# Three weight loads held back in the prologue, GpSimd's chunk products cut into pieces, and a new instruction order: delta-rule attention followed by SwiGLU on one core

## The chip, the core and the metric

The kernel runs on one core of a Trainium2 chip. Its time is device microseconds (us) from start to end of one execution. The time before is a median of 677.06 us over 3 runs (677.0, 677.06 and 680.48). The instructions are named by the engine that runs them: PE (TensorE), ACT (ScalarE), DVE (VectorE), POOL (GpSimd) and SP, which here only issues transfers.

## What is computed

```python
# q, k, v: (4, 8, 768, 48), beta: (4, 8, 768)
k_n = k / (norm(k, axis=-1) + 1e-6)
state = zeros((B, H, 48, 48))
for t in range(768):
    y[:, :, t] = q_t @ state                        # read before the write
    state = state + beta_t * outer(k_t, v_t - k_t @ state)
x = y.transpose(0, 2, 1, 3).reshape(3072, 384)
xn = x / sqrt(mean(x * x, axis=-1) + 1e-6) * rms_g
g = xn @ w_gate                                     # 384 x 1536
out = (g * sigmoid(g) * (xn @ w_val)) @ w_out       # 1536 x 384
```

The loads of w_gate, w_val and w_out find 64-bit numbers in HBM (the tiles that they land in are declared I64), so a weight tile is twice as large on the way in as in use and is converted to float32 on the chip.

## The kernel before

**Chunks.** The 768 steps are cut into 12 chunks of 64. For every chunk `prep(c)` builds the inverse of a triangular matrix of the keys, `recur(c)` uses it to get the chunk's outputs and the next state, and the feed-forward part (`ffn_plain` for chunks 0 and 1, `ffn` with fewer and smaller matmuls for the others) turns the normalized outputs into 256 rows of the result. `recur` of one chunk needs the state that the one before left. The feed-forward part depends on nothing later, so it is the filling that PE works through while the chain of small steps goes on beside it.

**Chunk 0** has nothing to hide behind. `invert(0)` (its merge levels are the two rounds n = 0 and 1 at lines 761 to 799) goes through transposes on DVE, 64-row matmuls mw (line 771) and mxt (line 790), and small products on ACT and DVE: the first level writes `wx` on DVE (line 784), the second on ACT (line 782). Then come mr0 (line 1102), the output matmuls pu (line 1082), the squares for the norm on ACT (line 1164), the root on POOL (line 1189), the scaling (lines 1200 and 1204), the turn of the result (line 1215) with its copy into xp1 (line 1224), and the first matmul of the feed-forward part (line 1287). Where the plan sees PE idle in this stretch, `run` puts matmuls of the identity in (line 1550), so that PE is not idle for long. Some 128-row work stands among the 64-row matmuls on purpose (`dense`, line 779).

**Weights.** `weights(first, last)` loads 18 tiles of 768 KB (n = 0 to 17; line 371) into seven landing buffers `raw`, and converts each: two ACT instructions (lines 469 and 470), two on DVE (lines 464 and 467). RAWS (line 291) says which buffer a tile lands in: n = 4, 5, 6 in raw 4, 5, 6; n = 7 to 9 in raw 0 to 2 again; n = 10 in raw 5. A buffer takes its next tile only when both ACT conversions of its last one have read it. Tiles 0 to 3 (HELD = 4) are planned before chunk 0's inverse; the rest after it. Raw 4 is held: a one-element POOL copy writes it from `wx[0]` (line 1502), and the load of tile 4 has to come after that write.

**Order.** Nothing is scheduled at run time. `P.add` numbers the operations in the order in which the program names them, with the engine, a planned duration and the tiles read and written; dependencies follow from these. The string ORDER (line 30) holds the order in which they are issued, two characters for each number. Every engine has its own queue, in order, and so has SP for the loads. The planned durations and start times no longer choose the order: they only place the fillers and hand out the eight PSUM banks, of which each matmul group holds one from its first matmul to its last reader.

**The long products.** For chunks 4 to 11 `prep` has `fast = False`: the scaling of the 128 x 1024 tile `at` by beta (line 846), the first shared product (line 871) and the sum (line 876) go to POOL, one instruction each. The steps of the inverse behind them (lines 893 and 899) run on DVE, as do the last operations of every feed-forward product (lines 1392 and 1399).

**The table.** A Silu of two numbers (line 404) stands in ACT's order ahead of all others, so that the table that Silu needs is loaded there.

Of the kernel before, what the change touches and what calls it, by code (L numbers as in the profile page):

```python
# [9 lines left out]
FP32 = mybir.dt.float32  # L10
U32 = mybir.dt.uint32
I64 = mybir.dt.int64
ALU = mybir.AluOpType
# [17 lines left out]
    "#.#'#-#$#3#)#4###,#/#&#0#>#`#W#C#^#a#T#_#X#U#k#(#Y#w#Z#d#l#b#n#m#e#o#V#t#H#c#+#2#@#u#f#*#[#]#v#r#x#S#p#y#R#z#?#1#{#E"  # L31
    "#M#|#q#=#}#i#s#~#j$##D$$%/$'$($%#A$&$*#%#J$.$/$)$+$0#F$,$1%0$I$2%1$-%2#G$7$6$5$3$8$;$N#I$<#h$X#N$C#K$=$D%4$>$9#P$?$:"
    "#L$S%5$B#O#g%8%7%6$4%;%:%9#B%=%<%>$@%G%?%@%H%Q$J%I%3%J%B%A%T%L%K$O%C%M%D%F%c%O%N%W%E%P%U&=%X&O&C%V&>#6$K#Q%Y%S$c$Q$P"
    "#9&G$E$^$R$A%Z&H$F%^%R$G%_&D$H$T$L&I'0&E%`%[&F$U&2&J%]$Y$m%a&K$d&1%b$Z&P&3%d&L%e$M&U&M%f$_&*%g&Q&)&N#:$V$h&R$[%h&0%i"
    "&V$r&S$`$a$W&W'1$w$]&Z&X&T$e$b&[&+$|%j$i%k&`%l&]$f%n&Y'2&4&a$g$s%m&e&^%o$j&,%p&b%%&-%q'_&_$k%r&.$n$l$o%w%v$x%*%s&j$u"
    "$t(3%x$z$}%y$y%t%z&c&/$v'+%u'O&%%|&5&&&$#<${'P(2%}'R'.$~&f%#%,$p%{&g'Q$q%$%~&h&6'S','/&'%'&#&d'-'T&((:'M&i'3#8'L'U#7"
    "'V'6#;%&&7&k'8'7'Z%+'Y(4&p%-#5'4'X'5%.'W'9(5&q(6%(&8)+'I':(7';&l%)'<'[&r'J&o),&m'='K&n&t'>&s(8)8&z'?)9'@)-'`']'E).*O"
    "'A&u):&A'N&{)l&v&|'B'^)o&y)p&w'C&~'D&x&}'a)m'#'b'c)n'F'd'G'$'e'f)q'('g'H)I'%)s)/)r(C'h)w'i&?(O(D')'j'&(G'*(E'k'')v(H"
    "(F(9'l*N(K'm(I&B)u'n(L&@'o)t(P(J'p(Q'q&9'r(R's(M(U(S't(N(V)0'u)1'w(Z(T'x)K(;'v([)y)2)x(W)E'|(]);(#(X)J(Y(`)3(^()){)<"
    "(*(a(')4)|($)F'~(e(_(%)z(b'}(()}'{)L(c(&)=(A(+)~'y(f*#(,(?*$'z*%(-&:(d(g*&)M(B(/(0*'*U(1(<(.(h*((@)N)O*V(i*)(k)P*P**"  # L40
    "(l&;*+(p(m)Q(=(n(q*Q*,(u(r*R(s(v(>*-*S(j(w*.(o*/&<*0(z*1*T)R*2(x,7*3({)S*4)k)T,8)>,:*6,9(t)j*8,;)?*5)U)5,<*7)V)6)G)W"
    "(y,=,>*W(~)Y,B(|)X,?)@)_,A(})Z)A)`)#,@)[)a*E)b)]*B)^)$)c*F)d*>)e)f+q)g,C)h)i,D)7*X*[)%*C)B*G*D*`)H,v*H*9*b*a)C*A*d)D"
    "*c+r)(*f+s*e)**Z,E,F*h)&*g*<,G*l*Y*@*=*i*n*:,H*m*j*?*r*o)'*I,},I*p*v,J))*;+.,w*q*s,K*t*J*^,L*M*w*x,M*K*u*~,N*L+w*y,O"
    "+t*_,P*]+&,x,~*k+x+u*z+'+v+0+#+(,y+2+1,z+)+**{+3,Q+/+6,{+$+y+4++,R+,+:*|+-+z+5+7*},|+<+%+;._+@+=+B+{+A+|+D,S+C+F,T+E"
    "+~.`,U+L+>+8+}+G.b.a+H+M,#.c,6+P-#,$+T+Q.d+I+R,%,V-$+N+J+S.e,*+U.f,&+O+]+V+9.h,'+K,+,(+W-),)+?.j,W+_.g+^+X,,.i+Z-',X"
    "+c,Y+Y,Z+[+`,-.l,5+a,[,.,^,/+e.<,_+b+d,0,`+g.>,]+f.k,1,2+i,3,4,m-++j-&--,j-,-%-*-/+h,f,g-1.m-0,n-.,i-U-2.n+l-7,k.o/A"
    "-9-8,c.p,l,o-:/B-3,p+k.q+m,e.r-4,h,a,b.s,q,d+n.t-5-=+p,s.=+o,u.u-A,t-(-;,r-6-?->.v-C.w-@.B-B.x.?.y-E-D.@/C.C-I-F-M-J"
    "-W-<-K-N-Q.z-O-G-X-Y-P-L-V/D-^-Z/E.D-[/J.A-b/F-].E-_-c.{-j-R-h-H-S/G-k-d-T.F1*.G.(-e.H.|.I-i-l.J.}-f-n.~.L.K1+/#-m-p"
    "-`-o-t-a-q1--u-x-r1,/$-|1.-y-v.M-g-z.Q-}.N/K.O-w.R.P-{-~-s1/.)/%.S.T.#.*.&11.$10.%/&.'14.U...^13/'15/I.V.+.,/+./.112"
    ".W/).0.4/(.-/M/*.X.Y.2.5.Z16.[171j/R.3/9.]/T/6/V/U.6/S.8/P19/7/H1:/X/W/0.918/Z/Y/3/_.:/[.;/a/`.71;/8/}/b/Q/g/L1</-1="  # L50
    "/./e/1/h/i/4/f1>/2/m1?/N/j1@/,/k/51A///:/n0g/;1B/o/O0d/l1i/<1C/u0h0e/@0f/q/>/=/v/c0#/?/d/r1p0%0$1D1q/w0j/x/p/~/y0k/]"
    "0l0'/^/s1E0&0)1k0(0i0-/z0*0m/{1l0+1m0.030n/|1n0/0,4404/t1)050o00090p1F06070q0:0;010r081o020C1G0?0<3Q0O0D0@0E0=1H0t0s"
    "3R1I3T3S0G1(3U0F0y0A0H0u3V0>0v0I0B0J3/0M3W0K0z0Q3X0L0P1J0w3Y0{3Z0W0U3]0N3[1K451L0S0R0X1M0V3_1N0[0T0|0x1Q0}0~1O1#0Y1$"
    "3^1%1&1R0]1'1P311z1r1|1{301x0Z1~1}1Y1_2$2#1T0`3`1U2%1]1[1v2*3a1a2&0a3b1`0_2,2'1^3c1s2+1S0b1y323d1u1V3e1b2-0^1W2H1c0c"
    "3f2.1w203g1Z3h1d1X21224;1t3i26233j33241h2728253k1e2@1f1g3l342<2(2A2J2)2B2=352C2/2I2L3m2K2>2D2946362P2:2E2M372N2?472F"
    "2T2G482O382Q493n2V2U2Z2W2]2;2[4=2R2_2^392a4A4:2`3o4C2c3:5y2g3O3<2d4>3;2b2X3=2h5z5|3p5{2k3>3P3?2o2l2e2i3@2p3D2w3q3E3F"
    "5}2S3A2q2j3B3r3G5~2m3C2n2f5V2Y6#2s2x2y6$2r2t6%2u2v6&3H2}6(3I2z3s6'4<3J3t2{3K3u3L3M3N3#6)4E2|4?3v4G5W3$4I3w3y3%4H3z2~"
    "3x6*3'3&4@4J4$4Q4#3(5X4%4F4M4R3|6,3}4p3*6-4K4,3~6+3+3)4L4+4N4D4(4S3,6.4'3.4W4T4*4-4B6/4X604[4&4U3-4r3{4]614)4Y6]624V"
    "6d4^634Z6[4d4s644.6c4O4`4_4P4/4e4h6542414t434a404i5Y4u664j5]5Z4k4f674|4q5[6e4b4v5_6^4x5^6k4w4l4}4~6_5`4m5#4n6l4y5$6i"
    "5(4o4c6`4g5&685)6a5*5a5'5b5.695+4z5,5c6:5d525-5e6f6b53568D5f5w5g5/5:57505l545;8E5h5%8G8F515B6;5i8H5<5x585=5j5m6<5n8%"  # L60
    "5k5o4{558I595>5C5D5p8J5@8K6=5?8O5H8M5E5q5A8N6>8L5r6j7~5s5t6?5F6g6@5u8P5v6h6A6m8$5G5I5K6o6D6B8#6q5J6C5N6E8Q5L5O6n6H6p"
    "7;5M908S6R6s6P6r6u6S8T6M8R6y9'6G5R6z6N6t6O8U5P6v6{5Q5S9(6T8V6|6Q7#8W6J6}6L6U7%6w5U7$8X5T7=6~6I8Y6K7'8Z9.6V6x7(6F8[7)"
    "948&7&8]7/6X6W7>7*7?6Z8^6Y738'7@708(74718_7775767+9)8)8`7G7<8*7C7H7A789*797O728+7:9+7B7D9,7,7I8,7-7M7P;O7J7E7U8a7N7Q"
    "8B7.7S9-7R8-:l7j8.7T7V8b7W7Y8/7F7K7^7X807Z:m7L7[7_:o817b828c7`:n877c83:p917f7d887a89:q847]858d868:7k7l7e:s8;:r8<7h8="
    ":u7g7p:w8e:t7i:v8>8?967n8@9/7m8A8f8g987o928h:y9:7s:x7q9<7r7v8i8l7t8k7w998j9;8m:z9c957u8C9=;N9>9D9@9E8x8n7z9?:{8u9A8z"
    "93:|7x9F8v8p:}9J8w9G8{9e8s9H:~7{7y;#9N7}8y9g9O9I8t;$9B8|7|;%9K8o9L9C978}9f;&9P8r8q;'9V9M9h9Q9R9o9S9Z9W9p8~9[:I;(9$9]"
# [161 lines left out]
def kernel(  # L228
# [207 lines left out]
    def weights(first, last):  # L436
# [14 lines left out]
        for n, (dst, src, keys) in list(enumerate(todo))[first:last]:  # L451
# [4 lines left out]
            dma(rdst, src, 2 + 2 * n, w=[("raw", i)], dur=0.7, work=3.06, after=WAFTER[n] if n < len(WAFTER) else 0.0)  # L456
# [21 lines left out]
    WAFTER = (4.0, 6.0, 11.0, 17.0, 20.0, 25.0, 28.0, 31.0)  # L478
# [321 lines left out]
    def prep(c):  # L800
# [44 lines left out]
        def scale():  # L845
            eng.tensor_tensor(out=at_, in0=at_, in1=bt[:, None, :].to_broadcast([128, W, W]), op=ALU.mult)  # L846

        P.add(e_, 1.27 if fast else 2.4, scale, pi, r=bkeys, w=[("at", 0), ("at", 1)])
# [21 lines left out]
        def share1():  # L870
            eng.tensor_tensor(
                out=pair, in0=at_[:, :, 0:W:2], in1=diag[:, None, :].to_broadcast([128, W, W // 2]), op=ALU.mult
            )

        def share2():
            eng.tensor_tensor(out=at_[:, :, 1:W:2], in0=at_[:, :, 1:W:2], in1=pair, op=ALU.add)

        def share3():
            for side in (0, 3):
                a1 = acc[0:64, side].rearrange("p i t -> p (i t)")  # L880
                eng.tensor_tensor(
                    out=a1[:, 1 : 1 + 34 * 15 + 1 : 34], in0=a1[:, 0 : 34 * 15 + 1 : 34], in1=diag[0:64], op=ALU.mult
                )

        P.add(e_, 1.17 if fast else 1.7, share1, pi, r=[("at", 0), ("at", 1)], w=xkeys)
        P.add(e_, 0.3 if fast else 0.5, share3, pi, r=[("at", 0), ("at", 1)], w=["acc"])
        P.add(e_, 0.69 if fast else 1.3, share2, pi, r=xkeys, w=[("at", 0), ("at", 1)])
        for j in range(0, W - 2, 2):
# [94 lines left out]
    def recur(c):  # L983
# [107 lines left out]
        def uk(h):  # L1091
            return [("u", bb, p) for bb in range(2) for p in h]
# [493 lines left out]
```

## Time and profile before

| | |
|---|---|
| median of the runs (lowest, highest) | 677.06 us (677.0, 680.48) |
| the profiled execution | 680.87 us; its span, first to last instruction, 679.2 us |
| busy, PE / DVE / ACT / POOL | 666.1 / 527.4 / 307.1 / 139.8 us |
| granted PE clock, mean | 0.992 |
| first matmul of the feed-forward part | at 46.25 us |
| end of PE's last matmul | 674.98 us |
| PE idle after 46.25 us | 0.26 + 1.63 + 0.17 + 1.31 + 0.18 + 1.49 us |
| L846 on POOL, 8 times | 2.36 us each |
| L871 and L876 on POOL, 8 times each | 1.76 and 1.30 us each |

In the views quoted below, a line of the timeline has the start in us, the time that the instructions took together, the engine, the line of the kernel, the operation, what it writes and reads, and how many were merged; in brackets stands the idle time before it and what ended that. SPq is SP's queue of transfers. A line of a table by stretch has the stretch, its length, the busy time and number of instructions of each engine, the granted clock of PE, and the share of time and rate of the transfers. A line of the waits has the waiting instruction, what it waited for, the total in us, how often and the longest. PE counts as busy with the identity matmuls too, so a busy PE in the first 46 us tells little.

### The profile page before, as it was taken

The page shows a single profiled execution, that of the slowest core. Times are in us where ns is not written, and L with a number is a line of the kernel's source. Part 1 is how long each engine was busy: PE and PEld are TensorE (multiplying, and loading weights), DVE is VectorE, ACT ScalarE, POOL GpSimd, SP SyncE. Part 2 cuts the span into 40 slices and gives each one's busy share as a digit, 9 for nine tenths or more (in the row PEclk, how much of TensorE's full clock was granted, in tenths as well). Part 3 has the DMA queues.
Part 4 walks back from the last instruction along what each step waited for, and adds up shares of the span by engine and source line. Part 5 has one row for each costly group of instructions (what it writes and reads, how often), then busy time and mean ns, then how long its engine had stood idle before and what let it go on. Part 6 is the DMA issues. An engine that isn't in the chain of part 4 may idle for free. (4 is left out here: it accounts for less than half of the span.)

```text
span 679.2 us, 23221 instructions
## 1 busy us (share of the span) xinstructions
PE 666.1 (98%) x10028; PEld 616.6 (91%) x10028; DVE 527.4 (78%) x1132; ACT 307.1 (45%) x744; POOL 139.8 (21%) x146
## 2 busy tenths in 40 slices
PE   8999999999999999999999999999999999999997
PEld 5688887887799999999899999999999989999997
DVE  5859978899899699589589689689679669956463
ACT  5566743133445345355255255255255254244330
POOL 2120341004321312312311403403403030000000
PEclk9979999999999999999999999999999999999999
DMA  9929752873732511831711650630721450040101
GB/s 219 277 73 259 251 117 28 156 131 89 125 44 52 103 23 28 142 60 26 122 33 25 114 91 4 117 56 16 125 51 23 68 98 3 10 72 2 24 1 25
DMA packets 216119, 55.73 MB, mean 82 GB/s; under 512 B 205200, under 2 KB 208272, under 8 KB 215696
## 3 DMA queue, kind: packets, MB, share of 16 engines
q1 hardware_dynamic: 214976, 54.05, 40.3%
q8 instruction: 79, 1.29, 0.8%
q10 hardware_dynamic: 1040, 0.20, 0.2%
q14 instruction: 24, 0.20, 0.1%
HBM read 42.94 MB, written 15.20 MB: 86 GB/s over the span
## 5 line engine op out<-in xcount | busy, mean ns | idle before, releaser
L1382 PE MATMUL bank<-xf,w_in 128*128 128x128 f32 x1440 | 180.0, 276 | 1.7 <-ACT tmp L1394 1.5
L1392 DVE TENSOR_TENSOR tmp<-tmp,bank 128x512 f32<-128x512 f32 x180 | 120.9, 684 | 67.2 <-PE bank L1382 54.3
L1382 PEld LDWEIGHTS bank<-xf,w_in 128*128 128x128 f32 x1440 | 169.7, 192 | 3.4 <-ACT tmp L1394 1.7
L1382 PE MATMUL bank<-xf,more 128*128 128x128 f32 x960 | 125.0, 277 | 1.8 <-DVE tmp L1392 1.6
L1382 PEld LDWEIGHTS bank<-xf,more 128*128 128x128 f32 x960 | 115.6, 192 | 4.3 <-DVE tmp L1392 2.0
L1394 ACT COPY tmp<-bank 128x512 f32<-128x512 f32 x120 | 68.7, 585 | 101.7 <-PE bank L1382 70.0
L899 DVE TENSOR_REDUCE acc<-acc 128x30 f32<-128x90 f32 (+4 forms) x150 | 70.9, 473 | 5.1
L1398 ACT ACTIVATE tmp<-tmp 128x256 f32<-128x256 f32 x120 | 48.1, 415 | 58.0 <-DVE tmp L1392 57.7
L597 POOL TENSOR_TENSOR knrm<-ksum,half 128x16 f32<-128x16 f32 x11 | 32.5, 2959 | 193.7 <-DVE ksum L576 193.7
L1439 PE MATMUL bank<-wo_sb,hf 128*128 128x192 f32 x360 | 63.7, 328 | 0.0
L1439 PEld LDWEIGHTS bank<-wo_sb,hf 128*128 128x128 f32 x360 | 58.1, 190 | 0.4
L1399 DVE TENSOR_TENSOR hf<-tmp 128x256 f32<-128x256 f32 x120 | 50.7, 445 | 7.4 <-ACT tmp L1398 6.9
L893 DVE TENSOR_TENSOR acc<-acc,at 128x60 f32<-128x60 f32 (+4 forms) x150 | 51.7, 345 | 2.8 <-DVE acc L899 0.5
L919 POOL COPY acc<-acc 128x128 f32<-128x128 f32 x40 | 19.3, 512 | 117.1 <-DVE acc L899 116.5
L1287 PE MATMUL bank<-xp,w_in 128*128 128x256 f32 x144 | 34.0, 383 | 0.3 <-ACT xp L1224 0.3
L1269 PE MATMUL bank<-wo_sb,hf 128*128 128x384 f32 x96 | 34.1, 488 | 0.0
L1287 PE MATMUL bank<-xf,w_in 128*128 128x256 f32 x144 | 33.4, 383 | 0.0
L846 POOL TENSOR_TENSOR at<-at,beta_b 128x1024 f32<-128x1024 f32 x8 | 18.9, 2362 | 65.2 <-DMA at<-dkk 65.2
L1287 PEld LDWEIGHTS bank<-xf,w_in 128*128 128x128 f32 x144 | 26.9, 190 | 5.2 <-issue 0.2
L1287 PEld LDWEIGHTS bank<-xp,w_in 128*128 128x128 f32 x144 | 26.7, 190 | 5.4 <-ACT xp L1224 0.5
L1239 DVE TENSOR_TENSOR xf<-xf 128x256 f32<-128x256 f32 (+1 forms) x70 | 25.6, 400 | 3.6 <-ACT xf L1224 3.2
L1448 DVE TENSOR_TENSOR tmp<-tmp,bank 128x192 f32<-128x192 f32 x30 | 10.5, 351 | 22.2 <-PE bank L1439 22.2
(204 smaller groups left out, 1025.8 us busy)
## 6 DMA issues: line engine op xcount, KB each, us to landing
at<-dkk SPq DMA_DIRECT2D x20, 256.0 KB, 3.6
vt<-in_v_dram SPq DMA_DIRECT2D x24, 192.0 KB, 4.8
out_dram<-tmp SPq DMA_DIRECT2D x48, 96.0 KB, 2.2
k<-in_k_dram SPq DMA_DIRECT2D x23, 192.0 KB, 4.8
more<-in_moe_w_gate_dram SPq DMA_DIRECT2D x4, 768.0 KB, 8.3
more<-in_moe_w_out_dram SPq DMA_DIRECT2D x4, 768.0 KB, 8.3
dkk<-kk SPq DMA_DIRECT2D x40, 64.0 KB, 2.6
q<-dq SPq DMA_DIRECT2D x20, 128.0 KB, 3.2
```

Source lines behind the costliest of these rows:

```text
L597: P.add("POOL", 2.95, lambda: nc.gpsimd.tensor_tensor(out=knrm[i2], in0=ksum[i2], in1=half, op=ALU.pow), pn, r=[("ksum", i2), "half"], w=[ ...
L893: nc.vector.tensor_tensor(out=acc[:, 1:3, 0:n, j + 2 : W].rearrange("p a i t -> p i a t"), in0=acc[:, old, 0:n, j : j + 2, None].to_broadc ...
L899: nc.vector.tensor_reduce(out=acc[:, new, 0:n, j + 2 : W], in_=acc[:, lo : lo + 3, 0:n, j + 2 : W].rearrange("p a i t -> p i t a"), axis=A ...
L1239: P.add("DVE", V(128 * n), lambda dst=dst, a=a, b_=b_, op=op: nc.vector.tensor_tensor(out=dst, in0=a, in1=b_, op=op), pxv, r=[("xp", 0)], ...
L1269: nc.tensor.matmul(po[p].t[:, 0:DM], hf[:, spot(f), 128 * p : 128 * p + 128], wo_sb[:, spot(f)], start=(f == f0), stop=(f == f1 - 1), skip ...
L1287: nc.tensor.matmul(ps.t[:, TOK * side : TOK * side + TOK], w_in[:, side, h_, 3 * t + i_, n : n + 128], x_[:, 2 * t : 2 * t + 2].rearrange( ...
L1382: nc.tensor.matmul(g.t[:, 128 * z : 128 * z + 128], fac[:, side, 128 * f : 128 * f + 128], xf[:, xs], start=(begin and z == 0), stop=False ...
L1392: P.add("DVE", V(512), lambda t=t, g=g: nc.vector.tensor_tensor(out=t, in0=t, in1=g.t, op=ALU.add), -1, r=[g], w=[tk], last=g)
L1394: P.add("ACT", A(512), lambda t=t, g=g: nc.scalar.copy(t, g.t), -1, r=[g], w=[tk], last=g)
L1398: P.add("ACT", A(256), lambda t=t: nc.scalar.activation(out=t[:, 0:256], in_=t[:, 0:256], func=ACTF.Silu), -1, w=[tk])
L1399: P.add("DVE", V(256), lambda t=t, f0=f0, p=p: nc.vector.tensor_tensor(out=hf[:, spot(f0) : spot(f0) + 2, 128 * p : 128 * p + 128], in0=t[ ...
L1439: nc.tensor.matmul(g.t[:, 0:192], a_[:, f], b_[:, f], start=(begin and f == 0), stop=(f == 5), skip_group_check=True)
```

## The change

1. **Holds.** Tiles 4, 5 and 6, and not 4 alone, are held, and until `wx[1]` of the second merge level is written, not `wx[0]`: three one-element POOL copies in place of one. The earliest planned times of the loads from tile 4 on (WAFTER) are dropped.
2. **Pieces.** The scaling and the first shared product of chunks 4 to 11 are cut into four POOL instructions of a quarter of the rows j each, the sum into two halves: 7 more instructions for each of 8 chunks. Chunks 2 and 3, whose products run on DVE, keep one instruction each.
3. **Planned durations.** Those of pu, ku, the squares, the root and the loads are changed. They move fillers and banks only.
4. **Order.** ORDER is a new string for the 2761 operations (2703 before). Read out by number and engine, its beginning says:

| queue | before | after |
|---|---|---|
| SP, after tile 3 and chunk 1's q | tiles 5, 6, 8, 4 (held), 7, 10, 9, 12 | tiles 8, 9, 4, 6, 5 (the three held), 7, 10, 11, 14 |
| ACT, from chunk 0's squares to x1 | two half conversions (one each of tiles 5 and 6, line 469) stand between the squares, the scaling and the copies into xp1 | one half conversion (tile 4) and one copy of chunk 1's turned keys stand there |
| ACT, the Silu of line 404 | ahead of chunk 0's merge levels, after the first conversion | behind the first seven Silus of the feed-forward part |
| ACT, from xp1 to the first Silu (line 1295) | 2 key copies, 5 half conversions, 4 other copies | 1 key copy, 6 half conversions |
| PE, chunk 0 | mw, mxt, mr0, pu, ku in this order | the same, with the turns of q and of chunk 1's keys at other places |
| PE, after the first feed-forward matmuls | the product of chunk 1's q with the state (line 1005) after 4 half products of the feed-forward part | after 9 of them and one down product |
| POOL | tile 4's copy, 2 roots of chunk 0, the scaling of chunk 1's keys | 3 copies, the scaling of chunk 1's keys, the 2 roots |

The diff without the strings of ORDER:

```diff
-            dma(rdst, src, 2 + 2 * n, w=[("raw", i)], dur=0.7, work=3.06, after=WAFTER[n] if n < len(WAFTER) else 0.0)
+            dma(rdst, src, 2 + 2 * n, w=[("raw", i)], dur=0.7, work=3.06 if n < HELD or n == 8 else 2.3, after=WAFTER[n] if n < len(WAFTER) else 0.0)
...
-    WAFTER = (4.0, 6.0, 11.0, 17.0, 20.0, 25.0, 28.0, 31.0)
+    WAFTER = (4.0, 6.0, 11.0, 16.0)
...
-        def scale():
-            eng.tensor_tensor(out=at_, in0=at_, in1=bt[:, None, :].to_broadcast([128, W, W]), op=ALU.mult)
-
-        P.add(e_, 1.27 if fast else 2.4, scale, pi, r=bkeys, w=[("at", 0), ("at", 1)])
+        def scale(j0, j1):
+            eng.tensor_tensor(out=at_[:, j0:j1], in0=at_[:, j0:j1], in1=bt[:, None, :].to_broadcast([128, j1 - j0, W]), op=ALU.mult)
+
+        pieces = (0, W) if fast else (0, 8, 16, 24, W)
+        for j0, j1 in zip(pieces, pieces[1:]):
+            P.add(e_, 1.27 if fast else 0.64, lambda j0=j0, j1=j1: scale(j0, j1), pi, r=bkeys, w=[("at", 0), ("at", 1)])
...
-        def share1():
+        def share1(j0, j1):
             eng.tensor_tensor(
-                out=pair, in0=at_[:, :, 0:W:2], in1=diag[:, None, :].to_broadcast([128, W, W // 2]), op=ALU.mult
+                out=pair[:, j0:j1], in0=at_[:, j0:j1, 0:W:2], in1=diag[:, None, :].to_broadcast([128, j1 - j0, W // 2]), op=ALU.mult
             )
...
-        P.add(e_, 1.17 if fast else 1.7, share1, pi, r=[("at", 0), ("at", 1)], w=xkeys)
+        for j0, j1 in zip(pieces, pieces[1:]):
+            P.add(e_, 1.17 if fast else 0.56, lambda j0=j0, j1=j1: share1(j0, j1), pi, r=[("at", 0), ("at", 1)], w=xkeys)
         P.add(e_, 0.3 if fast else 0.5, share3, pi, r=[("at", 0), ("at", 1)], w=["acc"])
-        P.add(e_, 0.69 if fast else 1.3, share2, pi, r=xkeys, w=[("at", 0), ("at", 1)])
+        pieces = pieces[::2] if len(pieces) > 2 else pieces
+        for j0, j1 in zip(pieces, pieces[1:]):
+            P.add(e_, 0.69 if fast else 0.72, lambda j0=j0, j1=j1: share2(j0, j1), pi, r=xkeys, w=[("at", 0), ("at", 1)])
...
-            P.add("PE", 0.49 * len(h), lambda h=h: pu(h), py, r=ptk + uk(h), w=gy, ps=gy, size=64 * len(h))
+            P.add("PE", 0.55 * len(h), lambda h=h: pu(h), py, r=ptk + uk(h), w=gy, ps=gy, size=64 * len(h))
...
-            P.add("POOL", 1.1 if c else 0.65, root, py, r=["half"], w=[(k_, i2, p) for p in h for k_ in ("ms", "rs")])
+            P.add("POOL", 1.1 if c else 0.85, root, py, r=["half"], w=[(k_, i2, p) for p in h for k_ in ("ms", "rs")])
...
-    t = raw[RAWS[HELD]].bitcast(FP32)[:, 0:1]
-    P.add("POOL", 0.2, lambda: nc.gpsimd.tensor_copy(out=t, in_=wx[:, 0, 0, 0:1]), 28, r=[("wx", 0)], w=[("raw", RAWS[HELD])])
+    for n in range(HELD, 7):
+        t = raw[n].bitcast(FP32)[:, 0:1]
+        P.add("POOL", 0.15, lambda t=t: nc.gpsimd.tensor_copy(out=t, in_=wx[:, 1, 0, 0:1]), 29, r=[("wx", 1)], w=[("raw", n)])
     weights(HELD, len(RAWS))
```

## The prediction, as it went on record

> **What bounds the kernel.** First the page and the waits of PE. PE is busy 98% of the span, the granted clock falls once, early, and PE waits seldom:
>
> ```profile
> PE 666.1 (98%) x10028; PEld 616.6 (91%) x10028; DVE 527.4 (78%) x1132; ACT 307.1 (45%) x744; POOL 139.8 (21%) x146
> PEclk9979999999999999999999999999999999999999
> PE bank L1382 <- DVE tmp L1392: 1.6, 1, 1.6
> PE bank L1382 <- ACT tmp L1394: 1.5, 1, 1.5
> PE bank L947 <- issue: 1.3, 1, 1.3
> PE bank L771 <- issue: 1.2, 1, 1.2
> ```
>
> Until 46.25 us PE follows chunk 0's chain; the rest of its work there is filling. From 46.25 to 674.96 it idles 5.04 us in all, so 623.7 us of matmuls stand in line there, and the change removes none of them. The time can move in three places only: the start of the feed-forward part, the 5.04 us, and 4.2 us of tail. So next I read the prologue's timeline and a table by stretch:
>
> ```profile
> 19.59 2.52 SPq L371 DMA_DIRECT2D wsum<-in_moe_w_gate_dram  x1
> 22.15 0.49 SPq L371 DMA_DIRECT2D wsum<-in_moe_w_val_dram  x1
> 22.74 0.43 SPq L371 DMA_DIRECT2D more<-in_moe_w_out_dram  x1
> 25.37 2.05 PE L790 MATMUL bank<-kk,x2bd 64*64 64x32 f32 x64
> 28.87 0.30 PE L771 MATMUL bank<-mt,m1bd 64*64 64x32 f32 x3
> 30.35 1.23 PE L771 MATMUL bank<-mt,m1bd 64*64 64x32 f32 x29 [1.17 <-issue]
> 32.65 3.63 PE L790 MATMUL bank<-kk,x2bd 64*64 64x32 f32 x64
> 46.25 1.56 PE L1287 MATMUL bank<-xp,w_in 128*128 128x256 f32 x6 [0.28 <-ACT xp L1224]
> ...
> 24.13:27.55 3.42, 3.42 (x100) 3.05 (x98) 3.39 (x8) 0.00 (x0) 0.71 (x1) 1.00 1.03 324
> 27.55:30.96 3.41, 2.24 (x57) 1.92 (x54) 3.26 (x7) 2.08 (x3) 2.33 (x2) 1.00 0.92 327
> 30.96:41.20 10.24, 10.24 (x200) 9.40 (x200) 4.42 (x9) 2.95 (x9) 0.00 (x0) 0.50 0.46 161
> ```
>
> In the middle of 32 equal matmuls of L771 PE stands for 1.17 us for nothing that a semaphore explains ("issue"). One packet of the instruction queue is in the trace just then: 16 KB, at 27.81 to 28.90 us. Transfers fill 1.03 and 0.92 of the time around it: tiles 5, 6 and 8, issued at 19.59 to 22.74. My reading: PE's next instructions were queued behind weights. In the stretch of the stall PE is busy 2.24 of 3.41 us, and for the next 10.24 us its clock is 0.50: the same 64 matmuls of L790 take 2.05 us before and 3.63 us after.
>
> **The parts, on the profiled execution's time** (680.87 us, which is the span of 679.2 and 1.67 around it).
>
> *Holds.* In the new order SP sends tile 8 as soon as raw 1 is converted, tile 9 when raw 2 is (about 25 us by ACT's rows), and then waits for `wx[1]`. So two tiles move where three did, and most of the time before 28 us is free for the instruction packet. I take the stall as gone: -1.2. If it goes, PE fills that stretch as it fills 24.13 to 27.55, where the clock stays 1.00; so the half clock goes as well. L790 3.63 to 2.05 is -1.6; mr0 (L1102, 64 instructions) 3.5 to the 2.0 that chunk 1's take at 89.86, -1.5; pu (L1082) 2.05 to 1.15 (chunk 1's at 94.59), -0.9; pieces around them -0.2. Together -4.2. Bounds: 0 if the clock falls anyway, -5.4 if both go.
>
> The added wait: behind tile 4 on SP stand tiles 6, 5, 7 and 10 and chunk 2's keys; who waits for tile 4 is ACT's conversion, which the new order puts in front of the scaling of chunk 0's output (L1204). `wx[1]` should be ready near 31 us, the POOL copies take 0.18 each. A tile issued into an empty queue lands about 4 us later (estimate: issue at 47.98, and in 50 to 52 us the transfers run at 391 GB/s, 2.0 us for each 768 KB). So tile 4 lands near 35 us, and ACT comes to it near 37. Hidden, with 1.5 to 2 us to spare; the others land every 2.0 us, for conversions after 41 us. POOL's two extra copies (0.36) fall in its 11.75 us of idle time ahead of L1189.
>
> *Order of the prologue.* ACT has one half conversion fewer (0.9) and one key copy more (0.55) between the squares and x1: -0.35. DVE's first steps come some 0.25 us later (the zeros for the queries' padding and the side sums stand behind the key sum); I take it as inside this term's error of 1 us.
>
> *The Silu of line 404* goes behind seven real ones, so the table load moves with it to the first of these. Now it is free: ACT waits for DVE's `gam` there.
>
> ```profile
> 12.47 1.28 ACT L404 ACT_TABLE_LOAD   x1
> 13.76 0.20 ACT L404 ACTIVATE rs<-mhalf 128x2 f32<-128x2 f32 x1
> ...
> 48.00:50.00 2.00, 2.00 (x69) 1.82 (x60) 0.84 (x1) 2.00 (x4) 0.00 (x0) 1.00 0.38 55
> 50.00:52.00 2.00, 2.00 (x11) 1.75 (x10) 1.86 (x5) 2.00 (x5) 0.00 (x0) 1.00 1.08 391
> ```
>
> Then it lands where ACT is busy without a gap (2.00 of 2.00). After the first feed-forward matmul PE has ten more feed-forward steps of 1.3 us and L664 (1.1), 14.1 us, before the product L1005, which needs both state copies and two banks; ACT has by then about 17 conversions and copies at 0.85 and ten small operations at 0.3 to 0.5, some 14.6 us, and 15.9 with the load. I take +1.3 (its row); bounds 0 if ACT is ahead, 2.0 if PE waits the whole difference. The Trainium skill ("ScalarE: Activation LUTs", What ACT_TABLE_LOAD costs) gives 1.28 us for the load and 1.38 more for a drain; here the next ACT instruction starts 1.29 us after the load, so the trace shows only the first. By the page's 2.66 the sum below would be 674.7.
>
> *Pieces.* The two waits of L1382 have one cause:
>
> ```profile
> 552.24 2.36 POOL L846 TENSOR_TENSOR at<-at,beta_b 128x1024 f32<-128x1024 f32 x1 [15.29 <-DMA at<-dkk]
> 552.31 2.58 DVE L1399 TENSOR_TENSOR hf<-tmp 128x256 f32<-128x256 f32 x1
> 555.40 1.37 DVE L1399 TENSOR_TENSOR hf<-tmp 128x256 f32<-128x256 f32 x1
> 557.44 0.82 PE L1382 MATMUL bank<-xf,w_in 128*128 128x128 f32 x5 [1.49 <-ACT tmp L1394]
> ```
>
> A DVE product of 0.42 us (median of 120) takes 2.58 while the long POOL product runs; ACT, then PE, wait behind it. At 176.67 the sums of L1347 stretch the same way beside L846, and PE waits 1.63. In pieces of 2.36/4 = 0.6 us DVE can get in between: -(1.63 + 1.49) = -3.1. Bounds: 0 if the lost turns come back elsewhere. Seven more starts for each chunk cost POOL at most 0.22 us each (two 16-element L881 take 0.44), 1.5 us in a period of 51 of which it is idle 37; they delay only the inverse of a later chunk. The 1.3 us at L947 is another "issue" wait; I leave it.
>
> *Planned durations* move fillers and banks: nothing measurable.
>
> **Sum:** -1.2 - 4.2 - 0.35 + 1.3 - 3.1 = -7.55; 680.87 - 7.55 = **673.3 us**. The median, 677.06, is 3.8 below the profiled execution, close to the 4.2 of the half clock, so I think that the runs at 677.0 had no such stretch: they would be at 676.7 by these terms. Against the median the gain is then only 3.7 us, 0.55%, just past the 0.5% (3.4 us) that a measurement of this kernel can tell from no change.
>
> **Rivals.**
>
> *The clock falls or the packet is late anyway.* Tile 9 may still be moving when the packet is due, and mr0 and pu are 64-row matmuls. Then 4.2 to 5.4 come back: 677.5 to 678.7. For it: the same kernel ran both at 677.0 and 680.5. Against: it fell right after the stall's stretch, and with 64-row work at full speed (24.13 to 27.55) it didn't. The Trainium skill ("TensorE: Matmul & The Clock Gate", What's actually happening) has the clock halve after an idle window of about 3.4 us; by that rule a stall of 1.17 us is no cause, and removing it brings back nothing of the 4.2, this rival's 677.5. The trace speaks against the rule: PE was never idle longer than 1.41 us before. Chance 0.15.
>
> *The pieces move no time:* DVE's lost turns are made up of more, shorter ones, or the new order has waits of its own of that size, of which the profile of before can show nothing. 673.3 + 3.1 = 676.4. For it: in 8 chunks only these two waits of PE came of 8 long products, so most are hidden. Against: both stretched products show the cause. Chance 0.18.
>
> *The hold blocks ACT,* the slower side: tiles 4, 6, 5 and 7 are issued together; if they land together, that is at 31.5 + 2 + 4 x 2.0 = 41.5 and not 35. For it: with a full queue the page's median to landing of a 768 KB tile is 8.3 us. ACT would stand before L1204 from 37 to 41.5, PE with it: +4.5, and a PE idle that long would lose the clock, +4.2: 682.0. It costs from a landing after 37 us, and makes the kernel slower than 680.4 from about 40. Against: in order of issue, tile 4 lands first. Chance 0.12.
>
> **How the numbers follow.** Forecast 0.52, own range 670.5 to 675.6: without the table's 1.3 and with L947's 1.3 gone it is 670.7; with 2.0 for the table and half of the pieces 675.6. About three quarters of it (0.40) lie under 673.7, where faster begins; the rest (0.12), the clock or packet (0.15) and the pieces (0.18) make same 0.45; the hold (0.12) and both small rivals at once (0.03; 673.3 + 4.2 + 3.1 = 680.6) make slower 0.15. The range takes the forecast's lower end and reaches over 676.4 and 678.7: 670.3 to 679.5; it leaves out the slower cases and little else.
>
> **What would show it.** The clock at 9 in all slices, no "issue" wait at L771; L1287's first start near 40.5; a table load of 1.28 us ahead of L1295 and a wait of 1 to 2 us at L1005; L846 32 times at 0.6 us, no L1399 over 1.1 us, and PE's waits at L1382 under 0.5 us. Wrong if PE starts the feed-forward part after 44 us, or if ACT's idle time names a DMA of tile 4.

## The result and the profile after

The changed kernel takes 682.51 us (median of 6 runs, 681.25 to 683.38); in the same rounds the kernel before took 677.56 us (6 runs, 677.0 to 680.58). The ratio is 1.0062, with an interval from 1.0038 to 1.0087: slower by 0.6%, where 0.55% faster was forecast. The profiled execution took 682.63 us, span 680.9. Before's profiled execution (680.87 us, mean clock 0.992) was one of its slower ones: of the 29 runs of before in the first group of rounds below, the 14 quickest (677.14 us or less) had a mean clock of 0.999 or 1.0. Lines of the changed kernel are 1 to 7 higher than before: L771 is L772, L1287 is L1293, L1382 is L1388.

The page's PE row and clock row, then the waits of PE:

```profile
PE 665.1 (98%) x10030; PEld 614.7 (90%) x10030; DVE 525.4 (77%) x1132; ACT 304.8 (45%) x744; POOL 153.7 (23%) x204
PEclk9989999999999999999999999999999999999999
```

```profile
PE bank L1145 <- issue: 3.2, 1, 3.2
PE bank L953 <- issue: 1.6, 1, 1.6
...
PE bank L1388 <- DVE pt L623: 1.1, 1, 1.1
```

The wait of 1.2 us at L771 and the two at L1382 are gone, as forecast, and the clock falls for a third of the time. But a longer "issue" wait stands elsewhere, in ku (L1145), and two waits come later, at L953 (1.6 us, where L947 had 1.3 before) and at L1388 (1.1 us, new). The prologue's timeline (SP, PE and ACT):

```profile
28.05 2.05 PE L772 MATMUL bank<-mt,m1bd 64*64 64x32 f32 x64
31.20 0.37 SPq L372 DMA_DIRECT2D hf<-in_moe_w_out_dram  x1
36.17 0.63 PE L1145 MATMUL bank<-u,k 64*64 64x48 f32 x26
37.01 0.89 ACT L470 ACTIVATE xf<-hf 128x768 f32<-128x768 f32 x1
40.04 0.89 PE L1145 MATMUL bank<-u,k 64*64 64x48 f32 x38 [3.24 <-issue]
45.86 1.56 PE L1293 MATMUL bank<-xp,w_in 128*128 128x256 f32 x6 [0.59 <-ACT xp L1230]
```

L772 now runs through. Tile 4 (`hf`) is issued at 31.20 us, tiles 6, 5 and 7 right behind it at 31.66, 32.17 and 32.66. ACT converts tile 4 at 37.01 without waiting: the rival that blocks ACT is false. PE stops after 26 of ku's 64 matmuls. The table by stretch (same columns as in the prediction) has the clock's answer:

```profile
37.18:40.59 3.41, 0.55 (x35) 0.55 (x38) 1.43 (x4) 1.45 (x3) 1.75 (x4) 1.00 1.05 396
40.59:44.01 3.42, 3.42 (x26) 2.30 (x17) 0.00 (x0) 0.00 (x0) 0.00 (x0) 0.50 0.21 76
```

PE is busy 0.55 of 3.41 us, and then its clock is half for one stretch. The feed-forward part starts at 45.86 us, 0.4 earlier than before and not 5.7.

What came before the stall is in the view of the transfers. In 33.40 to 37.60 us, and in 37.60 to 38.80:

```profile
q1 hardware_dynamic: 715, 1.61, 99.4%
...
q8 instruction: 1, 0.02, 5.6%
```

From 33.40 to 37.60 only the queue of SP's loads moves (715 packets). In the next 1.2 us comes the one instruction packet, 37.67 to 38.75 us. PE goes on 1.3 us behind it.

**The theories.** A: PE's instructions come in packets of 16 KB, one for 256 of them (the trace has 20060 matmuls and weight loads of PE and 132 semaphore and drain instructions, 20192 in all, and 79 packets). PE asks for a packet when it starts on the block before it; a packet that has to stand behind weight tiles is late. Counted in the trace, the stall begins after 1217 of PE's instructions, and the "issue" waits at L771 before (705) and at L953, L1388 and L1011 after (10177, 5313, 16833) all lie at the same place of a block (193 over a multiple of 256, give or take one). PE passed 961 at 33.40 us; the packet for 1217 started 4.3 us later, behind tiles 4, 6, 5 and 7 that the three holds had set free together. B: the stall is ku's own, or of the new order, whatever the holds do.

### The profile page after: what moved, and what is told of

The parts are those of the page before. It is cut to its first block, busy times and chain, and to the rows that moved or that the text cites. A ratio compares the mean times of both kernels' runs of the same rounds, so it can differ in the third digit from the quotient of the medians.

```text
span 680.9 us, 23270 instructions
## 1 busy us (share of the span) xinstructions
PE 665.1 (98%) x10030; PEld 614.7 (90%) x10030; DVE 525.4 (77%) x1132; ACT 304.8 (45%) x744; POOL 153.7 (23%) x204
## 3 DMA queue, kind: packets, MB, share of 16 engines
q8 instruction: 78, 1.28, 0.8%
## 4 chain that ended last, share of the span: by engine, by line
PE 69%; DVE 2%; issue 1%; DMA 1%; ACT 0%; SPq 0%; ACTq 0%; DVEq 0%
PE bank L1388 38%; PE bank L1445 19%; PE bank L1011 2%; PE bank L553 2%; PE bank L1088 1%; PE bank L1074 1%; PE bank L530 1%; PE bank L1221 1%; PE bank L1145 1%; PE bank L973 1%; PE bank L953 1%; DVE xf L1245 1%; DMA out_dram<-tmp 1%; DVE xp L1437 0%; DVE tmp L1398 0%
## 5 line engine op out<-in xcount | busy, mean ns | idle before, releaser
L1388 PE MATMUL bank<-xf,w_in 128*128 128x128 f32 x1440 | 180.8, 277 | 2.1 <-DVE pt L623 1.1
L1388 PEld LDWEIGHTS bank<-xf,w_in 128*128 128x128 f32 x1440 | 170.0, 192 | 4.5 <-issue 1.3
L1388 PE MATMUL bank<-xf,more 128*128 128x128 f32 x960 | 124.6, 277 | 0.0
L1388 PEld LDWEIGHTS bank<-xf,more 128*128 128x128 f32 x960 | 115.8, 192 | 2.2 <-DVE acc L899 0.4
L1405 DVE TENSOR_TENSOR hf<-tmp 128x256 f32<-128x256 f32 x120 | 48.4, 423 | 9.0 <-ACT tmp L1404 8.6
L847 POOL TENSOR_TENSOR at<-at,beta_b 128x256 f32<-128x256 f32 x32 | 25.6, 829 | 96.0 <-DMA at<-dkk 81.9
L1245 DVE TENSOR_TENSOR xf<-xf 128x256 f32<-128x256 f32 (+1 forms) x70 | 29.6, 449 | 9.0 <-ACT xf L1230 8.5
L1293 PE MATMUL bank<-xp,w_in 128*128 128x256 f32 x144 | 33.3, 382 | 0.6 <-ACT xp L1230 0.6
L925 POOL COPY acc<-acc 128x128 f32<-128x128 f32 x40 | 17.7, 476 | 69.6 <-DVE acc L905 69.5
L1293 PE MATMUL bank<-xf,w_in 128*128 128x256 f32 x144 | 32.7, 381 | 0.0
L1293 PEld LDWEIGHTS bank<-xp,w_in 128*128 128x128 f32 x144 | 26.9, 190 | 5.8 <-ACT xp L1230 0.8
L1293 PEld LDWEIGHTS bank<-xf,w_in 128*128 128x128 f32 x144 | 27.1, 190 | 4.8
```

The costliest lines, as they stand in the source:

```text
L1245: P.add("DVE", V(128 * n), lambda dst=dst, a=a, b_=b_, op=op: nc.vector.tensor_tensor(out=dst, in0=a, in1=b_, op=op), pxv, r=[("xp", 0)], ...
L1293: nc.tensor.matmul(ps.t[:, TOK * side : TOK * side + TOK], w_in[:, side, h_, 3 * t + i_, n : n + 128], x_[:, 2 * t : 2 * t + 2].rearrange( ...
L1388: nc.tensor.matmul(g.t[:, 128 * z : 128 * z + 128], fac[:, side, 128 * f : 128 * f + 128], xf[:, xs], start=(begin and z == 0), stop=False ...
L1405: P.add("DVE", V(256), lambda t=t, f0=f0, p=p: nc.vector.tensor_tensor(out=hf[:, spot(f0) : spot(f0) + 2, 128 * p : 128 * p + 128], in0=t[ ...
```

## The experiments

Times are medians of 4 to 12 runs, of up to five rounds; the ratio is to the kernel before in the same rounds (677.2, 677.6, 677.85 and 676.8 us in the four groups), 0.001 of it is 0.68 us. The other columns are of the profiled execution: start of the feed-forward part, longest "issue" wait ahead of it, time at half clock ahead of it, PE's idle time after it, and the time that PE's work after it takes without that (us). The work is the same 9370 matmuls in every kernel but pieces_hold_root, which has 8 more.

| kernel | median | ratio (interval) | start | issue | half | idle | work |
|---|---|---|---|---|---|---|---|
| before | 677.56 | 1 | 46.25 | 1.17 | 10.2 | 5.04 | 623.7 |
| changed | 682.51 | 1.0062 (1.0038, 1.0087) | 45.86 | 3.24 | 3.4 | 5.00 | 625.8 |
| late_release | 677.36 | 0.9993 (0.9975, 1.0012) | 40.49 | none | 0 | 3.71 | 625.8 |
| silu_back | 677.97 | 1.000 (0.998, 1.002) | 46.47 | 2.86 | 6.8 | 1.94 | 624.4 |
| whole | 682.75 | 1.0077 (1.0048, 1.0106) | 44.5 | 2.08 | 3.4 | 5.41 | 627.0 |
| before_pieces | 673.91 | 0.9942 (0.9922, 0.9963) | 46.43 | 2.79 | 6.8 | 1.92 | 623.7 |
| late_release_silu_back | 675.94 | 0.9976 (0.9959, 0.9994) | 40.58 | none | 0 | 3.90 | 624.8 |
| before_holds | 685.21 | 1.0120 (1.0096, 1.0144) | 51.37 | 2.82 | 3.4 | 5.67 | 624.5 |
| pieces_late | 685.22 | 1.0118 (1.0093, 1.0144) | 49.81 | none | 0 | 4.95 | 627.3 |
| sixtyfour_more | 679.14, one run | | 47.16 | 2.73 | 6.8 | 1.38 | 624.8 |
| pieces_hold_root | 676.12 | 0.9984 (0.9952, 1.0015) | 41.43 | 0.35 | 0 | 2.24 | 626.4 |
| one_hold | 676.50 | 0.9972 (0.9951, 0.9993) | 42.59 | 2.50 | 0 | 2.29 | 624.4 |
| one_hold_silu_back | 675.35 | 0.9972 (0.9958, 0.9986) | 43.97 | 2.50 | 3.4 | 2.01 | 623.7 |
| one_hold_whole | 680.74 | 1.0059 (1.0031, 1.0087) | 44.33 | 2.50 | 3.4 | 4.37 | 626.2 |

### The stall

**late_release**: the order of the changed kernel, but the copies that free the buffers come later.

```diff
 POOL
-  the 3 hold copies
   the scaling of chunk 1's keys
+  the 3 hold copies
 ACT
-  first conversion of tile 4 (ahead of the scaling L1210)
   the copies into xp1
+  first conversion of tile 4
```

> The changed kernel, with its three POOL copies behind the scaling of chunk 1's keys (about 34 us and not 31), the loads of tiles 4, 6, 5 and 7 behind them, and tile 4's first conversion behind the copies into xp1, so that ACT doesn't wait for it. Theory A (PE's instruction packet, due when PE passes one block boundary and needed at the next, stood behind the four tiles that the hold let go at 31.2 us): the packet is fetched before the burst, the 3.2 us wait at L1145 falls under 0.5 us, the clock stays at 1.00, the feed-forward part starts at 40.5 to 41.5 us, and the time is 682.5 - 4.7 = 677 to 678.5. Theory B (PE runs through blocks of small matmuls faster than instructions can come, whatever the loads do): the wait at L1145 stays at 2.5 us or more and the time at 682 to 683.

Measured: 677.36 us, 5.1 under the changed kernel. The timeline of PE, and from 33 to 35 us the view of the transfers:

```profile
36.12 1.11 PE L1144 MATMUL bank<-u,k 64*64 64x48 f32 x64
...
40.49 0.70 PE L1292 MATMUL bank<-xp,w_in 128*128 128x256 f32 x2 [0.65 <-ACT xp L1229]
```

```profile
DMA packets 1, 0.02 MB, mean 8 GB/s; under 512 B 0, under 2 KB 0, under 8 KB 0
```

The instruction packet has the queues for itself (it starts at 33.54 us, 0.2 us after PE passes instruction 961, and lands at 34.49), ku runs through in 1.11 us, and the feed-forward part starts at 40.49 us. Time and start are as A has them, to 0.01 us. So the place of the burst makes the stall.

**sixtyfour_more**: the update L791 of the second half is issued twice.

```diff
-                    for u, g in units:
+                    for u, g in list(units) * (2 if c == 0 and n and p else 1):
                         nc.tensor.matmul(xp_.t[low(g), W * u : W * u + W], X[low(g), p, u], wx[low(g), p, u])
```

> The changed kernel with the 64 matmuls of the last update of the inverse (L791) issued twice for the second half of chunk 0; the second time writes the same values again. Theory A (the stall is at a fixed count of PE's instructions, where the next block has not come): the stall comes 64 matmuls earlier in the program, so in the 64-row products ahead of ku (L1088), at the same count of instructions, and is between 2 and 3.5 us. Theory B (ku, L1145, waits for something of its own that the profile doesn't name): the stall stays at L1145 after about 26 of its matmuls.

The expectation had the size wrong: the update of one half has 32 matmuls, not 64. The timeline:

```profile
36.50 0.66 PE L1088 MATMUL bank<-u,pt 64*64 64x48 f32 x26
39.89 0.35 PE L1088 MATMUL bank<-u,pt 64*64 64x48 f32 x3 [2.73 <-issue]
```

With 32 matmuls more the stall comes 32 matmuls earlier, after 26 of the second half of pu and not 26 of ku, and again after instruction 1217. It belongs to a count of instructions and not to ku, so B's first form is false. (Its time, 3.4 us under the changed kernel for more work, is one run: no wait at L953 and L1388 is in it.)

**one_hold**: the changed kernel with before's single hold, and tiles 5, 6 and 8 early again. The plan then has no identity matmul behind ku, where the changed kernel has four.

```diff
-    for n in range(HELD, 7):
-        t = raw[n].bitcast(FP32)[:, 0:1]
-        P.add("POOL", 0.15, lambda t=t: nc.gpsimd.tensor_copy(out=t, in_=wx[:, 1, 0, 0:1]), 29, r=[("wx", 1)], w=[("raw", n)])
+    t = raw[RAWS[HELD]].bitcast(FP32)[:, 0:1]
+    P.add("POOL", 0.2, lambda: nc.gpsimd.tensor_copy(out=t, in_=wx[:, 0, 0, 0:1]), 28, r=[("wx", 0)], w=[("raw", RAWS[HELD])])
 SP
-  tiles 8, 9, 4, 6, 5, 7, 10
+  tiles 5, 6, 8, 4, 7, 9, 10
```

> The changed kernel without the three holds: one hold on wx[0] and the loads of tiles 5, 6, 8, 4, 7 in the order of the kernel before; all else is the changed order. Theory A (the burst of four tiles at 31 us is what makes the packet of ku late): the stall in ku goes, one of 1 to 1.5 us near 29 us at L772 may come back, the feed-forward part starts between 40.5 and 46 us, and the time is 677 to 681, below the changed kernel's 682.5. Theory B (the packet of ku is late whatever the holds do): the stall of 2.7 to 3.3 us at ku stays and the time is 682 to 684.

Measured: 676.5 us. Neither theory was right throughout: the stall stays (2.50 us, B's place; three tiles from 31.11 us on still stand ahead of the packet, which starts at 37.00), but the time is even below A's. The table by stretch says why the stall costs no clock in the profiled execution:

```profile
37.88:41.29 3.41, 1.76 (x47) 1.71 (x48) 1.09 (x4) 1.32 (x4) 1.28 (x3) 1.00 0.32 117
```

The stall is split over two stretches, PE is busy 0.75 of the first and 0.52 of this one, and the clock doesn't fall. That is not so in most runs: in 9 of the 12 the mean clock was 0.994 to 0.997. Of the 7.2 us between the two profiled executions 3.3 are gained up to the start of the feed-forward part, and 2.50 of these are the four identity matmuls (L1557, 40.86 to 43.36 us in the changed kernel, at half clock). The rest is gained at 183 to 204 us (1.3) and 318 to 345 us (2.5), where the waits at L1388 and L953 are shorter or gone.

**before_holds**: the kernel before with the three copies on `wx[1]` and the loads in the order 8, 4, 6, 5, 7. The order is otherwise before's, but the plan sees the hold later and puts 18 identity matmuls behind ku, where before has four.

> The kernel before with the three holds on wx[1] and the loads in the changed kernel's order, long POOL products whole, table load early. Theory A (the instruction packets are late whenever weight tiles queue ahead of them): the stall at L771 (29 us) goes and one of 2.5 to 3.3 us comes in ku (L1144) near 37 to 40 us, the clock is half behind it, the feed-forward part starts after 45 us, and the time is 677.5 to 682. Theory B (the holds do what the prediction said, and another part of the new order makes the stall): no stall, start near 40.5, 672 to 674.

Measured: 685.21 us. As A said, the stall at L771 is gone and one of 2.82 us stands in ku. ACT also waits, as the third rival has it, since it converts tile 5 ahead of the scaling (L1203) here; the changed order had avoided that. The timeline of ACT and PE:

```profile
41.11 0.90 ACT L468 ACTIVATE more<-wsum 128x768 f32<-128x768 f32 x1 [4.29 <-DMA wsum<-in_moe_w_gate_dram]
41.91 0.71 ACT L1203 ACTIVATE yn<-bank,rs 128x192 f32<-128x192 f32 x2
...
40.78 8.84 PE L1550 MATMUL bank<-ident 128*128 128x512 f32 x18
49.45 0.82 PE L1214 MATMUL bank<-ident,yn 128*128 128x128 f32 x6
```

But the scaling is done at 42.62 us, and PE comes to the turn of the result (L1214) only at 49.45, behind the 18 identity matmuls. So it is these that put the start off to 51.37 us, and not ACT's wait; the 3 us past A's range are theirs.

**All kernels together.** Whether the packet for 1217 is late hangs on when the burst of tiles comes, and not on the number of holds. In the four kernels that free the buffers after PE has passed 961 (late_release, late_release_silu_back, pieces_late, pieces_hold_root) this packet starts 0.2 to 0.4 us after that point; in the other nine (before left aside) 3.0 to 4.4 us after it, and each has the stall, of 2.08 to 3.24 us. Four of the nine have a single hold like before's: one_hold, its two variants, and before_pieces (below), whose POOL, ACT, DVE and SP do the same in the same order as before's in the first 60 us. Its timeline of PE, and the view of its transfers from 36.5 to 37.8 us:

```profile
40.07 1.31 PE L1144 MATMUL bank<-u,k 64*64 64x48 f32 x36 [2.79 <-issue]
```

```profile
q1 hardware_dynamic: 38, 0.04, 8.7%
```

Most of the 16 DMA engines are idle there: 8.7% is the time of 1.4 of them. The load packets that are left follow one another up to 37.82 us, and at 37.82 the instruction packet starts. That is what a packet does that stands behind the remaining loads of one engine; the trace doesn't name the engine. Before has no stall at this boundary in its profile: the stall at L771 and the half clock bring PE to 961 only at 37.73 us, when the packet is already moving (37.51 us).

### The table

**silu_back**: the changed kernel with the Silu of L404 again behind the negated betas, far ahead of the real ones.

```diff
 ACT
   negated betas
+  Silu of two numbers
...
   the 7th Silu of the feed-forward part
-  Silu of two numbers
```

> The changed kernel, with the Silu of line 404 (the table load) back ahead of chunk 0's merge levels, behind the negated betas where ACT is idle. If the table load in front of the first feed-forward Silu costs PE what the prediction took, 682.5 - 1.3 = 681.2. If PE, which starts that part 5 us later than forecast, is behind ACT anyway, at most the 0.5 us that L1011 waits for ACT at 60.6 us: 682.0 to 682.5.

**late_release_silu_back** has both edits:

> The changed kernel with both mends at once: the landing buffers are given free behind the scaling of the keys, near 34 us, and the Silu that loads the table is back behind the negated betas. Theory A (two separate losses: a late instruction packet that costs about 5, and the table load with the small waits behind it, about 2 to 4 by the two runs before, of which some was the same clock): the losses add, 673 to 675.5 us, the feed-forward part starts near 40.5 us, no issue wait above 1 us before it, no wait of L1010 for ACT. Theory B (the table's early load gave its gain only by making the clock fall less often, so there is one loss and not two): 676.5 to 677.5, as with the late release alone.

**one_hold_silu_back** is one_hold with this edit:

> The changed order without its holds (as one_hold), and the Silu that loads the table back behind the negated betas. Theory A (the load's place costs what was forecast, 1.3 us, and the small waits behind it): 674 to 675.3 against 676.5, no wait of L1010 for ACT. Theory B (the gain of 4.5 us that the same edit gave in the changed kernel was the clock falling in fewer runs): 676 to 677, no gain, since most of the clock's loss is gone without the holds.

Measured: 677.97, 675.94 and 675.35 us. Against the same kernel with the late load that is -4.5, -1.4 and -1.15 us by medians, and -4.2, -1.2 and 0.0 by the ratios. The wait of L1010 for ACT's state copy is gone in all three. So the load's place costs 0 to 1.4 us where it was tried outside the changed kernel. late_release_silu_back lies between both expectations, and one_hold_silu_back 0.05 us above its A. silu_back lies below both of its own: in the changed kernel the gain was larger. Its stall still stood (2.86 us), but 4 of 12 runs had a mean clock of 0.999 or 1.0 where all runs of the changed kernel had 0.994 to 0.997. What moved the clock there is open.

### The pieces

**before_pieces**: the kernel before, with the long products in pieces only (the diff's part 2).

> The kernel before with nothing changed but the pieces, all pieces of a product at the place of the product. By the prediction's term -3.1: 674.4, and the two waits of L1382 beside L846 (1.63 and 1.49 us) under 0.5 us each. By its rival, shorter lost turns that are more in number: 677.5 within 1 us, with the waits of the same sum at other places.

**whole**: the changed kernel, with the products in one instruction each.

```diff
-        pieces = (0, W) if fast else (0, 8, 16, 24, W)
+        pieces = (0, W)
```

> The changed kernel with POOL's products of chunks 4 to 11 whole again, each at the place of its first piece. If the pieces are worth the 3.1 us of the prediction in this order, 685.6; if DVE waits as long behind four pieces as behind one product (a wait of DVE's sums of L1245 beside four pieces in the trace says so), 682.5 within 1 us.

**one_hold_whole** is the same edit in one_hold:

> The changed order without its holds (as one_hold), GpSimd's long products of a chunk whole again. Theory A (in the new order no PE wait stands behind a whole product, so the pieces are worth nothing here): 676 to 677.3. Theory B (the pieces are worth their 3 us in any order, and the changed kernel's loss of the clock covered it): 679 to 680.5, and one or two waits of PE at L1386 for DVE or ACT of 1.4 us or more.

Measured: the pieces bring 3.3 us in the old order (673.91), 4.2 in the new one without holds (680.74 to 676.5), and 0.2 in the changed kernel (3.9, 5.9 and 1.0 by the ratios). In before_pieces the two waits at L1382 are gone, and no wait of PE behind DVE or ACT is over 0.3 us after the start: the forecast's side, and not its rival's. whole comes out where its second expectation has it. B of one_hold_whole is right in size (0.24 us above its range), at another place than it named. Its timeline of POOL, DVE and PE around the longest wait of PE:

```profile
266.80 2.41 POOL L845 TENSOR_TENSOR at<-at,beta_b 128x1024 f32<-128x1024 f32 x1 [7.41 <-DMA at<-dkk]
266.92 2.57 DVE L1435 TENSOR_TENSOR tmp<-xp,hf 128x256 f32<-128x256 f32 x1
...
274.76 1.63 PE L1443 MATMUL bank<-wo_sb,xp 128*128 128x192 f32 x6 [2.86 <-DVE xp L1435]
```

A DVE sum takes 2.57 us beside the whole product, where it takes 0.95 beside the pieces in one_hold; PE waits 2.86 us, in one stretch of 3.41 (busy 0.20 of it), and the clock is half for the next. "whole" has the same wait at 272.9 us. So the changed kernel gains 4.2 us there too by its trace, and loses 2.3 at 321 to 336 us: the packet of L953 comes 1.59 us late, and then DVE's turns stand between POOL's pieces. Its timeline:

```profile
328.37 3.36 POOL L847 TENSOR_TENSOR at<-at,beta_b 128x256 f32<-128x256 f32 x4 [14.98 <-DMA at<-dkk]
328.45 3.42 DVE L1245 TENSOR_TENSOR xf<-xf 128x256 f32<-128x256 f32 x4
```

Four DVE products of 0.42 us (their median) take 3.42 beside four pieces of 0.84, as if each waited for one piece: 1.7 us lost (3.42 - 4 x 0.42), not much under the 2.15 (2.57 - 0.42) beside one long product. Behind them stands the wait of L1388 for DVE (1.07 us, at 333.40). Another 1.35 us of the difference are the prologue's stall, 2.08 us in the profile of "whole" and 3.24 in that of the changed kernel; no instruction of the pieces lies there, and whether that is chance is open.

### Two tries at a better kernel

**pieces_late**: before_pieces, with the one hold behind the scaling of the keys and tiles 4, 6, 8, 7 behind it.

> The kernel before with the products in pieces; its one hold is given free behind the scaling of the keys (near 34 us) and tiles 6 and 8 are sent behind tile 4, so that only tile 5 moves from 20 to 34 us. Theory A: neither of the two packets is late; no issue wait above 1 us before the feed-forward part, which starts near 40.5 us in every run; 672 to 674 us, and fewer runs near 677 than with the pieces alone (673.9). Theory B (tiles 6 and 8 come late and ACT or PE waits for them): a wait for a DMA of tile 6 or 8 of 1 us or more and 675 or more.

**pieces_hold_root**: before_pieces, with the hold behind the first root, and tiles 4, 8, 7 behind it; tiles 5 and 6 stay early.

> The kernel before with the products in pieces; its one hold is given free behind the first root of GpSimd (near 36 us), tile 8 is sent behind tile 4, and tiles 5 and 6 stay early, since ACT converts them first. Theory A (late instruction packets behind weight tiles are the whole loss of the prologue): both packets land in time in every run, no issue wait above 1 us before the feed-forward part, which starts near 40.5 us; 672 to 674 us, and no run above 675.5, where the pieces alone had two of nine. Theory B (some other tile, 4, 7 or 8, then comes late to ACT): a wait of ACT for a DMA of 1 us or more before 55 us, and 675 or more.

Both took the stall ahead of the start away, as A has it, and neither was quicker than before_pieces. pieces_late (685.22 us) is its B: ACT waited 7.46 us for tile 6, ahead of the copies into xp1, and 24 identity matmuls stood behind ku until the start at 49.81 us. Two "issue" waits further on (2.65 us up to 89.82, 1.35 up to 300.37) were each followed by a stretch of 3.4 us at half clock. pieces_hold_root (676.12 us) starts the feed-forward part at 41.43 us and pays 2.0 us of that back, by neither theory. The plan, which sees the hold later, has put eight identity matmuls (L1555, 2.00 us at 50.62) behind the start, where before_pieces has none. All but one of its 12 runs were above 675.5, two of them far (682.22 and 685.1; their clock was 0.992 and 0.989). The best kernel remains before_pieces: 0.58% under the kernel before.

## Why the prediction was wrong

**The holds: the step that failed.** "So two tiles move where three did, and most of the time before 28 us is free for the instruction packet. I take the stall as gone." The term was -5.4 (-1.2 and -4.2). For that packet the step is right: it lands at 26.1 to 27.1 us in the seven kernels with three holds, and none of them waits at L771. But the step looked at one packet, in one execution. The five other kernels that send tiles 5 and 6 early, as before does, wait at L771 for 0 to 0.35 us, so most of the 1.17 us belonged to that execution. And the next packet, for the block that starts in ku, was asked for near 33.40 us, 2.2 us after the holds had let four tiles go together: PE stands 3.24 us there, and the clock is half for 3.4 us. That stall was not new with the three holds (2.50 us in one_hold, 2.79 in before_pieces); they left it where it was, one block behind the stall that they removed. The mechanism was in the text ("PE's next instructions were queued behind weights"); the burst that the change itself makes was in it too, as the rival's "issued together", but only as a danger to ACT.

**What the parts are worth** together is open in part. The holds, by one_hold against the changed kernel and with the four identity matmuls that go with them, are worth +6.0 us, of which the profiles place 3.3 in the prologue and put the rest into waits at 183 to 204 and 318 to 345 us. Why those grow with the holds is not settled. Nor do the losses add: a later release, an early load of the table, or no three holds take 5.1, 4.5 and 6.0 us off the changed kernel, each alone, and the first two together 6.6.

**The first rival** ("the packet is late anyway", 0.15) came nearest to the cause, at 677.5 to 678.7; it priced the old stall coming back and not a longer one at the next packet, and nothing of what follows. **The third** ("hold blocks ACT", 682.0) had nearly the time, by luck: its mechanism isn't there, since tile 4 landed before 37.01 us. That in order of issue tile 4 lands first was right.

**The half clock** goes when the stall goes (0 us of it in the profiles of late_release and pieces_hold_root), so it did hang on the stall. The rest of its step, that a stall of this kind costs 4.2, was too simple: stalls of 2.5 to 3.2 us cost 0, 3.4 or 6.8 us of half clock, by where they fall (below).

**The table**: +1.3 forecast, 0 to 1.4 measured outside the changed kernel. The load stands ahead of L1301 with 1.28 us, as said; the wait at L1011 is 0.5 and not 1 to 2.

**The pieces**: -3.1 forecast; -3.3 alone, -4.2 in the new order without holds, -0.2 in the changed kernel. The size was right and "in pieces DVE can get in between" too; that rival 2's "more, shorter" turns would also come true beside them was not expected (L1388's 1.07 us). L847's pieces take 0.73 us in the median and 0.83 in the mean, where 0.6 was forecast: a quarter takes more than a fourth of 2.36 us even with DVE idle, and up to 1.84 us beside DVE's operations.

**The order of the prologue** (-0.35): late_release starts at 40.49 against the 40.5 that was forecast with it, so the term holds within its error of 1 us. That it fits to the hundredth is luck, since late_release also has a conversion of 0.9 us behind the copies into xp1 that the changed kernel has ahead of them. What the terms took as fixed is PE's work behind the start, 623.7 us before: the same 9370 matmuls take 625.8 us in the changed kernel, and 624.4 in silu_back and one_hold. Why is open.

**The planned durations** were put at nothing, and behind ku the changed kernel has the same four identity matmuls as before. But the fillers that the plan places are not nothing: where an experiment moved the hold in the plan, they took up to 8.8 us behind ku (before_holds).

**The range** (670.3 to 679.5) left out the slower cases; they had 0.15. Each was priced from one late transfer, while the change altered what every later transfer stands behind.

## What to carry to other kernels

A hold that empties a queue for one moment fills it at another: before moving transfers, list every instruction packet of the busy engine near them and ask what will stand ahead of each, the ones after the release above all. An "issue" wait at a fixed count of instructions is such a packet; a block of small matmuls lasted 3.2 us here and left no time for a queue. A stall seen in one profiled execution may be another's next stall, so look at a second one before pricing it. And test the parts of a change one by one: the pieces alone beat both kernels, and with the other parts nothing of it was left.

## What the runs showed of the hardware

**Instruction packets.** With empty queues a packet takes 1.0 us (33.54 to 34.49 us in late_release), and 1.1 us among the loads of the changed kernel (37.67 to 38.75): it is late because it starts late. PE goes on 1.3 to 1.5 us after a late one has landed (38.75 to 40.04, 320.63 to 322.08 us). In the changed kernel the block ahead of the stall (instructions 961 to 1217) lasted 3.2 us, 33.40 to 36.58. The Trainium skill ("Runtime: NRT & Kernel Launch", Instruction fetch mechanics) has blocks of 16 KiB, or 256 instructions, and calls the cost of crossing a boundary mostly hidden. The traces agree on the block; hidden it is not where weights queue: 3.24, 2.86, 2.82, 2.79, 2.73, 2.50 (in three kernels) and 2.08 us at one boundary.

**The clock.** Cut into stretches of 3.41 us from the instant at which the clock changes, PE's busy share tells most: after all 10 stretches at full clock with a share from 0.16 to 0.48 (in eight executions) the next one ran at half clock; between 0.51 and 0.70 it did after 3 (0.56, 0.61, 0.66) and did not after 16, of which 8 are the first stretch at full clock of their execution; above 0.70 it never did. As the place of the stretches differs from run to run, one stall of 2.5 us can cost nothing (one_hold) or 3.4 us at half clock (one_hold_silu_back, busy 0.28). The Trainium skill ("TensorE: Matmul & The Clock Gate", What's actually happening) says that this window runs freely and is 3413 ns, with which the traces agree; but the clock falls here after windows in which PE was busy up to two thirds, not idle.
